# Pooled keys and left-over attention of batches 2 to 7 turned through DRAM and VectorE blocks

## The chip, the cores and the metric

The kernel runs on one core of one Trainium2 chip (trn2). The metric is the device time of one execution in microseconds (us). The core's engines are TensorE (PE, matmuls and the turning of 128x128 blocks; PEld is its loading of weights), VectorE (DVE), ScalarE (ACT), GpSimd (POOL) and SyncE (SP, which only issues DMAs). Each engine takes its own instructions in order; semaphores hold one back until what it reads is there.

## What is computed

q, k and v have 8 batches, 8 heads, 576 positions and 64 numbers a head. Keys and values are pooled by eight to 72, then softmax attention, and its output (576 x 512 a batch) goes through a gated MLP whose gate mixes positions.

```python
k_p = k.reshape(B, H, Sp, pool, D).mean(axis=3)      # pool = 8, Sp = 72
v_p = v.reshape(B, H, Sp, pool, D).mean(axis=3)
attn = softmax(q @ k_p.T / sqrt(D))                  # with + 1e-09 under the fraction
x = (attn @ v_p)                                     # heads side by side: 576 x 512
h = gelu_tanh(x @ w_in); u, v = h[..., :512], h[..., 512:]
v_s = w_sg @ (layer_norm(v) * g_ln) + b_sg
out = x + (u * v_s) @ w_out
```

## The kernel before, in words

The work of a batch is cut into steps named by a letter, each a Python generator (one function `step_X`); every call of it gives out the instructions up to its next `yield`. Which call comes when is written out by hand in four tables of tokens, `PROLOGUE`, `FIRST`, `PERIOD` and `LAST` (lines 23 to 69): `T1+1` is the next call of step T, group 1, of the batch after the one that the table stands for. `PERIOD` is run for batches 2 to 6, `FIRST` for 1 and `LAST` for 7 (lines 955 to 959). A token of a step that is already through gives out nothing. The order of the tokens is the order of every engine's instructions, DMA issues on SP's queue included (lines 961 to 966).

The steps, for batch b and group g or part i:

- A, B load k and v (`load_kv`, line 314), E loads the eight left-over positions of each head's 72 pooled ones (`load_left`, line 334), C loads q (`load_q`, line 348), each as several DMAs on SP's queue.
- K0 and K1 sum k by eight (line 396, tile `kp`), K2 sums the left-overs (tile `lp`), then turns `kp` with two and `lp` with one 128x128 transpose on TensorE into PSUM (lines 420 and 422) and scales the result into `kbd` on ScalarE (lines 430 and 431). P does the values.
- Q turns q in 32x32 blocks on VectorE (line 501), from a tile `qraw` into a tile `qT`, two of each.
- S multiplies q with `kbd` (line 514), takes the maximum, the exponentials and the sum and divides; GpSimd then copies the columns of the left-over keys into `el` (line 564).
- T turns the 128 main columns with five transposes on TensorE (helper `turn`, line 161), ScalarE rounds the result to `ah` (line 600) and VectorE makes the rest `al` (line 607). L does the same with the 64 columns of `el`: five transposes, four copies of 32x576 (line 580), two subtractions (line 587), into `lt`.
- V multiplies attention with the values (eight matmuls), H is the v half and U the u half of the first MLP matrix, W the mixing of positions (28 matmuls of 288 columns), G the combinations for a product scheme of batches 1 to 6, O the second matrix (in those batches seven products of 12 matmuls, each followed by VectorE's addition, line 841), Z turns the output and stores it.

Matmul operands are split into a rounded part and the rest; all matmuls of the steps stand at line 126. PSUM has four buffers, taken with `take()` and given back with `give()`; a step that takes one waits for the instruction that last read it.

Of the kernel before, what the change touches and what calls it, by code (L numbers as in the profile page):

```python
# [40 lines left out]
S2+0 H1+0 r0 S2+1 V0+0 S1-15 r0 V2+0 Q0+2 P2+1 P2+0 S3+1 W1-12 W0-11 r0 Z2-1 S3+1 r0 P2+1 S2-9 r0 r1 H1+0 H3+0 H3+0
O3-1 H2+0 Z1-1 r1 H3+0 P0-2 H1+0 O3-1 W0-6 H2+0 S3+1 H4+0 H4+0 O3-1 r1 S2+1 H0+0 H3+0 H2+0 H4+0 H2+0 r1 U2+0 Z3-1 H1+0
H3+0 H0+0 P2+1 P1-2 S3+1 S1-1 r3 C1+2 H1+0 H3+0 H4+0 Z3-1 H0+0 H4+0 U3+0 S1+1 S3+1 W1-1 H1+0 H4+0 U1+0 U2+0 Z2-1 H0+0
V1-21 U1+0 W0-17 E0+2 H4+0 U0+0 K0+2 S2+0 H0+0 U3+0 H4+0 H0+0 K1+2 r3 W1+0 W0+0 W1+0 A1-3 U0+0 T0+1 W0+0 r3 r3 L0+1
# [946 lines left out]
```

## Time and profile before

| what | value |
|---|---|
| runs (us) | 557.1, 557.34, 558.71; median 557.34 |
| the profiled execution, span from its first to its last instruction | 554.8 us |
| its own time beside the span | not given on the page; the runs' median lies 2.5 us over the span |
| TensorE | 542.7 us busy, 98% of the span, 3753 matmuls |
| VectorE, ScalarE, GpSimd | 415.6, 374.5 and 307.3 us busy |
| DMA | 46.34 MB, nearly all from SP's queue |
| granted TensorE clock | 1.00 in every slice of the span |

Matmuls are pipelined: the listed duration of one (298 ns for 288 columns) overlaps with that of the next, so the cost of a group is read from one start to the next start. The time of an engine that another one waits for is read from the lists of waits and the chain of work that ended last, the share of busy time is an average over all stages.

### The profile page before, as it was taken

Reading aid. Unit: us, or ns where it says so; the run is one execution under the profiler, and the core shown is the slowest. Engines: PE = TensorE matmul, PEld = TensorE weight load, DVE = VectorE, ACT = ScalarE, POOL = GpSimd, SP = SyncE. Lnnn points to the kernel's source line nnn. Section 1 sums busy time; section 2 is a strip of 40 time slices with the busy share of each in tenths; the row PEclk is TensorE's granted clock in tenths of the full one; section 3 lists DMA queues with packets and bytes.
Section 4 is the critical chain, followed back from the end, with each engine's and each line's share of the span. In section 5 each row is a group of like instructions: output and inputs, shape, how many; then the busy total and the mean of one; then the engine's idle time right before and its main releaser. Section 6 shows DMA issues by size and latency. Waiting matters only on the chain.

```text
span 554.8 us, 10369 instructions
## 1 busy us (share of the span) xinstructions
PE 542.7 (98%) x3753; PEld 513.9 (93%) x3753; DVE 415.6 (75%) x592; ACT 374.5 (68%) x981; POOL 307.3 (55%) x365
## 2 busy tenths in 40 slices
...
PEclk9999999999999999999999999999999999999999
...
GB/s 251 326 220 218 190 66 55 54 128 63 98 1 78 116 22 106 24 108 108 12 117 43 68 107 90 40 77 116 24 108 22 108 1 1 1 42 45 2 1 86
DMA packets 161603, 46.34 MB, mean 84 GB/s; under 512 B 149072, under 2 KB 149072, under 8 KB 161552
## 3 DMA queue, kind: packets, MB, share of 16 engines
...
q8 instruction: 29, 0.48, 0.4%
q14 instruction: 22, 0.18, 0.1%
...
## 4 chain that ended last, share of the span: by engine, by line
PE 65%; DVE 11%; ACT 6%; issue 1%; POOL 1%; DVEq 0%
PE ps L126 62%; PE ps L161 3%; ACT e L538 2%; DVE e L556 1%; DVE vk L694 1%; DVE nmax L519 1%; DVE kp L396 1%; DVE bst L683 1%; ACT L709 1%; ACT L538 1%; DVE xmem L689 1%; ACT xmem L678 1%; DVE qT L501 1%; DVE vbl L476 1%; DVE left L673 0%
## 5 line engine op out<-in xcount | busy, mean ns | idle before, releaser
L126 PE MATMUL ps<-wsh,vk 128*128 128x288 f32 x512 | 97.8, 298 | 1.4 <-DVE al L607 1.4
L126 PE MATMUL ps<-xhlk,wih 128*128 128x288 f32 x512 | 89.9, 298 | 0.0
L126 PE MATMUL ps<-wih,xhlk 128*128 128x512 f32 x256 | 84.6, 398 | 0.0
L126 PEld LDWEIGHTS ps<-wsh,vk 128*128 128x128 f32 x512 | 77.9, 188 | 2.2 <-PE ps L126 2.2
L126 PEld LDWEIGHTS ps<-xhlk,wih 128*128 128x128 f32 x512 | 75.6, 189 | 0.9
L538 ACT ACTIVATE e<-ps,nmax 128x72 f32<-128x72 f32 x240 | 73.0, 338 | 0.2
L694 POOL TENSOR_TENSOR vk<-xmem,vk 128x512 fp32r<-128x512 f32 x32 | 43.4, 1369 | 43.5 <-DVE nmax L519 24.8
L126 PEld LDWEIGHTS ps<-wih,xhlk 128*128 128x128 f32 x256 | 48.1, 188 | 10.7
L126 PE MATMUL ps<-wsl,vk 128*128 128x288 f32 x256 | 57.4, 295 | 0.0
L126 PE MATMUL ps<-xhlk,wil 128*128 128x288 f32 x256 | 55.0, 296 | 0.0
L538 ACT ACTIVATION_READ_ACCUMULATOR e<-ps,nmax 128x1 f32 x240 | 54.0, 225 | 0.0
L841 DVE TENSOR_TENSOR xmem<-ps,xmem 128x576 f32<-128x576 f32 x42 | 31.5, 755 | 26.8 <-PE ps L126 26.6
L126 PE MATMUL ps<-wil,xhlk 128*128 128x512 f32 x128 | 50.5, 395 | 0.0
L639 POOL TENSOR_TENSOR xhlk<-xmem,xhlk 128x576 fp32r<-128x576 f32 x32 | 45.4, 1434 | 1.9 <-ACT xhlk L637 1.5
L126 PE MATMUL ps<-gk,woh 128*128 128x288 f32 x224 | 46.3, 298 | 0.0
L686 POOL TENSOR_TENSOR rstd<-mv,eps 128x1 f32<-128x1 f32 (+1 forms) x40 | 7.9, 197 | 68.8 <-DVE ssum L547 35.7
L126 PE MATMUL ps<-kbd,qT 128*128 128x144 f32 x320 | 44.6, 287 | 1.1 <-ACT qT L496 0.8
L126 PEld LDWEIGHTS ps<-kbd,qT 128*128 128x128 f32 x320 | 42.2, 190 | 2.7 <-ACT qT L496 1.0
L126 PEld LDWEIGHTS ps<-wsl,vk 128*128 128x128 f32 x256 | 42.2, 188 | 0.0
L126 PEld LDWEIGHTS ps<-xhlk,wil 128*128 128x128 f32 x256 | 41.1, 188 | 0.0
L771 POOL TENSOR_TENSOR vk<-umem,vk 128x576 fp32r<-128x576 f32 x24 | 34.1, 1422 | 10.2 <-ACT vk L769 10.2
L785 POOL TENSOR_TENSOR umem<-umem 128x576 f32<-128x576 f32 x24 | 34.3, 1433 | 9.2 <-DVE umem L755 8.3
...
## 6 DMA issues: line engine op xcount, KB each, us to landing
...
```

The source lines that it names most:

```text
L126: nc.tensor.matmul(o, lhsT, rhs, start=start, stop=stop, **flags)
L161: nc.tensor.transpose(ps[:rows, i * P:(i + 1) * P], src(i), ident if i < NT - 1 else swap)
L396: nc.vector.tensor_reduce(out=o, in_=t.rearrange("p a (r d) -> p a d r", r=POOL), axis=AX.X, op=ALU.add)
L476: nc.vector.scalar_tensor_tensor(vbl[r, :, D * h:D * h + D], vp[r], 1.0 / POOL, vbh[r, :, D * h:D * h + D].bitcast(F32), op0=ALU.mult, op1 ...
L501: nc.vector.transpose(qT, st.pop(("q", b, g)).rearrange("p a i -> p (a i)"))
L538: nc.scalar.activation(e[:, i, h], slots[i][:, h], AF.Exp, bias=nmax[:, i, h:h + 1], **acc)
L639: nc.gpsimd.tensor_tensor(xhl[:, 1, g], x32[:, g], xhl[:, 0, g].bitcast(F32), op=ALU.subtract)
L686: nc.gpsimd.tensor_tensor(rstd, mv[:, 1:2], eps[:n, 1:2], op=ALU.add)
L694: (nc.gpsimd if i < NT - 1 else nc.vector).tensor_tensor(lo, vg, hi.bitcast(F32), op=ALU.subtract)
L771: nc.gpsimd.tensor_tensor(lo, x, hi.bitcast(F32), op=ALU.subtract)
L785: nc.gpsimd.tensor_tensor(x, p, q, op=ALU.subtract)
L841: nc.vector.tensor_tensor(x, ps[:, :, 0:HALF], x, op=ALU.add)
```

## The change

For batches 2 to 7 (`KEYS_TE` and `LEFT_TE` name the two batches that stay as they were) the turns of `kp`, `lp` and `el` on TensorE are left out. The tile is stored to DRAM, loaded back so that 32x32 blocks lie as VectorE's block transpose needs them, and turned there. K2 then has two stores, four loads, one VectorE transpose of 128x288 and the same scalings, from SBUF; it has five calls in place of three. L has two stores, two loads, one VectorE transpose of 96x576, the same four copies on ScalarE, and its two subtractions go to GpSimd; it has six calls in place of four. Neither takes a PSUM buffer any more. The tile that comes back from DRAM in K2 lies in the buffer of `el`.

To make room, q is loaded and turned in place in three buffers (`qbuf`), where there were two raw and two turned ones, and the constant `apart` lies in the first columns of `bbc`, which is loaded once `apart` is no longer needed.

All four tables are written anew. The first five lines of `PROLOGUE` and the first seven tokens of the sixth are the same. In the diff the other tables are left out but for `PERIOD`.

```diff
 PERIOD = """
...
+S1+1 H0+0 V0+0 C3+1 S0+1 Q2+1 H0+0 H2+0 S1+1 V2+0 V3+0 H2+0 H0+0 V1+0 S0+1 S1+1 H3+0 H0+0 H4+0 H4+0 H2+0 U0+0 P1+1
+H0+0 H4+0 H2+0 S1+1 S1+1 H1+0 H3+0 H0+0 P0+1 Q3+1 H4+0 S2+1 H1+0 U0+0 T0+1 H2+0 S2+1 H1+0 A1+2 T0+1 H3+0 S0+1 S3+1
+U1+0 S3+1 T0+1 H4+0 S2+1 S2+1 C0+2 A0+2 H1+0 S3+1 H1+0 H3+0 S3+1 U2+0 P2+1 H3+0 H4+0 U3+0 S2+1 H4+0 H2+0 H4+0 H1+0
+U3+0 S3+1 H3+0 W1+0 U1+0 K0+2 P2+1 U2+0 L0+1 W1+0 W0+0 P2+1 L0+1 W0+0 B0+2 K1+2 G1+0 W3+0 L0+1 G0+0 W2+0 G0+0 P2+1
+L0+1 W3+0 G1+0 E0+2 L0+1 W2+0 L0+1 G1+0 T1+1 G2+0 G2+0 V0+1 T1+1 T2+1 T1+1 O0+0 V1+1 G2+0 G3+0 V0+1 O1+0 C1+2 G4+0
+K2+2 T2+1 T2+1 G2+0 V2+1 O0+0 V1+1 G3+0 G2+0 Q0+2 K2+2 G3+0 T3+1 K2+2 Q1+2 B1+2 O0+0 T3+1 T3+1 W1-5 G4+0 C2+2 V3+1
+W0-4 O0+0 G4+0 O0+0 O0+0 V1+1 V3+1 O2+0 G4+0 O1+0 K2+2 V2+1 O2+0 G4+0 O1+0 K2+2 O1+0 Z1+0 V0+1 V2+1 S0+2 S0+2 Z1+0
+V3+1 Z0+0 O0+0 O0+0 Z3+0 Z0+0 Z2+0 Z2+0 Z3+0
 """.split()
 """.split()
...
@@ -99,11 +96,19 @@
     REC_SB = ((0, 0), (0, 1), (0, 2), (0, 3))
     MUL_POOL = ((0, 0), (0, 1), (0, 2), (0, 3))
     LO_W = ()
+    KEYS_TE = (0, 1)
+    LEFT_TE = (0, 1)
     W_POOL = ()
 
     const = ctx.enter_context(tc.tile_pool(name="const", bufs=1))
     per = ctx.enter_context(tc.tile_pool(name="per", bufs=1))
     psum = ctx.enter_context(tc.tile_pool(name="psum", bufs=1, space=bass.MemoryType.PSUM))
+
+    dram = ctx.enter_context(tc.tile_pool(name="dram", bufs=1, space=bass.MemoryType.DRAM))
+
+    fark = [dram.tile([9 * 32, P], F32, name=f"fark{n}") for n in range(2)]
+
+    farl = [dram.tile([S, H * JL], F32, name=f"farl{n}") for n in range(2)]
 
     turns = {}
 
@@ -130,7 +135,8 @@
     nc.vector.memset(kbd, 0.0)
     ident = const.tile([P, P], F32, name="ident")
     make_identity(nc, ident)
-    apart = const.tile([P, P], F32, name="apart")
+    bbc = const.tile([P, S], F32, name="bbc")
+    apart = bbc[:, 0:P]
     nc.gpsimd.tensor_copy(apart.rearrange("p (a j) -> p a j", a=2), ident.rearrange("p (j a) -> p a j", a=2))
     mhalf = const.tile([P, 1], F32, name="mhalf")
     nc.gpsimd.memset(mhalf, -0.5)
@@ -170,8 +176,11 @@
     wth = const.tile([P, S], F32R, name="wth")
     wtl = const.tile([P, S], F32R, name="wtl")
     nc.gpsimd.memset(wtl.bitcast(F32)[TAIL:2 * TAIL], 0.0)
-    bbc = const.tile([P, S], F32, name="bbc")
     gcol = const.tile([P, DF2 // P], F32, name="gcol")
+
+    eraw = const.tile([96, S], F32, name="eraw")
+    nc.gpsimd.memset(eraw[32:64], 0.0)
+    qbuf = const.tile([P, 3, S], F32, name="qbuf")
 
     st = {}
 
@@ -356,7 +365,7 @@
                 load(t[:, :, h], q[b, 2 * g + h].rearrange("(t p) d -> p t d", t=6))
             st["q", b, g] = t
             return
-        t = per.tile([P, S // 32, 32], F32, name="qraw", tag=f"qraw{g % 2}")
+        t = qbuf[:, (G * b + g) % 3].rearrange("p (k i) -> p k i", i=32)
         for h in range(2):
             sv = q[b, 2 * g + h].rearrange("(t j) (f i) -> f j t i", j=32, i=32)
             for f in range(2):
@@ -415,21 +424,38 @@
         psum8(lp[r], st["left", b][r], "left", b)
         yield
         kp = st.pop(("kp", b))
+        if b not in KEYS_TE:
+            back = fark[b % 2]
+            load(back[0:2 * P].rearrange("(a p) c -> p a c", p=P), kp.rearrange("p (a h) d -> p a (h d)", h=2))
+            load(back[2 * P:2 * P + 32], lp[96:P].rearrange("p h d -> p (h d)"))
+            yield
+            kt = per.tile([P, 9, 32], F32, name="kt", tag="el")
+            for f in range(4):
+                load(kt[32 * f:32 * f + 32], back.rearrange("(k j) c -> j k c", j=32)[:, :, 32 * f:32 * f + 32])
+            yield
+            kt = kt.rearrange("p k i -> p (k i)")
+            nc.vector.transpose(kt, kt)
+            yield
+            scale_k(b, kt[:, 0:2 * P], kt[:, 2 * P:])
+            return
         bank, ps = take()
         for a in range(2):
             nc.tensor.transpose(ps[:, 0, P * a:P * (a + 1)],
                                 kp[:, 2 * a:2 * a + 2].rearrange("p h d -> p (h d)"), ident)
         nc.tensor.transpose(ps[:, 1, 0:P], lp.rearrange("p h d -> p (h d)"), ident)
         yield
-        main = ps[:, 0, 0:2 * P].rearrange(*(("p (a l j) -> p a l j",) if b in BY_PE else ("p (a j l) -> p a l j",)), a=2, l=2)
+        scale_k(b, ps[:, 0, 0:2 * P], ps[:, 1, 96:P])
+        give(bank)
+
+    def scale_k(b, main, rest):
+        main = main.rearrange(*(("p (a l j) -> p a l j",) if b in BY_PE else ("p (a j l) -> p a l j",)), a=2, l=2)
         split_k = kbd.rearrange("p (a l) c -> p a l c", l=2)
-        rest = ps[:, 1, 96:P].rearrange("p (j g) -> p g j", g=G)
+        rest = rest.rearrange("p (j g) -> p g j", g=G)
         c = D ** -0.5 / POOL
         for h in range(2):
             r = slice(D * h, D * h + D)
             nc.scalar.mul(split_k[r, :, :, JL + JM * h:JL + JM * (h + 1)], main[r], c)
             nc.scalar.mul(kbd[r, :, LEFT[h]:LEFT[h] + JL], rest[r], c)
-        give(bank)
 
 
     vb = {b: vraw[:, 2 * (NT - 1) * DF2:].bitcast(F32).rearrange("p (g n) -> p g n", g=G) for b in WHOLE}
@@ -484,7 +510,7 @@
         st["vl", b] = vl
 
     def step_Q(b, g):
-        qT = per.tile([P, S], F32, name="qT", tag=f"qT{g % 2}")
+        qT = qbuf[:, (G * b + g) % 3]
         if b in NATURAL:
             t = st.pop(("q", b, g))
             n = S // 6
@@ -498,7 +524,8 @@
             give(bank)
             st["qT", b, g] = qT
             return
-        nc.vector.transpose(qT, st.pop(("q", b, g)).rearrange("p a i -> p (a i)"))
+        st.pop(("q", b, g))
+        nc.vector.transpose(qT, qT)
         st["qT", b, g] = qT
         yield
 
@@ -566,6 +593,28 @@
 
     def step_L(b, _):
         el = st.pop(("el", b))
+        if b not in LEFT_TE:
+            back = farl[b % 2]
+            n = (NT - 1) * P
+            load(back[0:n].rearrange("(t p) k -> p t k", p=P), el[:, 0:NT - 1])
+            load(back[n:S], el[P - TAIL:P, NT - 1])
+            yield
+            raw = eraw.rearrange("p (k i) -> p k i", i=32)
+            for gp in range(2):
+                load(raw[64 * gp:64 * gp + 32], back.rearrange("(k i) n -> i k n", i=32)[:, :, 32 * gp:32 * gp + 32])
+            yield
+            nc.vector.transpose(eraw, eraw)
+            yield
+            src = [eraw[64 * gp:64 * gp + 32] for gp in range(2)]
+            for gp in range(2):
+                lt = st["lt", b, gp] = per.tile([96, S], F32R, name="lt", tag=f"lt{gp}")
+                for c in (0, 2):
+                    nc.scalar.copy(lt[32 * c:32 * c + 32], src[gp])
+            for gp in range(2):
+                yield
+                lt = st["lt", b, gp]
+                nc.gpsimd.tensor_tensor(lt[32:64], src[gp], lt[64 * gp:64 * gp + 32].bitcast(F32), op=ALU.subtract)
+            return
         bank, ps = take()
         ps = ps.rearrange("p a n -> p (a n)")
         turn(ps, lambda i: el[:, i])
```

## Rows read from the trace of the kernel before

**Rows 1.** The page, busy time of each engine and the granted clock in 40 slices.
```profile
PE 542.7 (98%) x3753; PEld 513.9 (93%) x3753; DVE 415.6 (75%) x592; ACT 374.5 (68%) x981; POOL 307.3 (55%) x365
...
PEclk9999999999999999999999999999999999999999
```

**Rows 2.** Busy time by stretch: from:to, length, then each engine's busy us (instructions), clock, DMA share.
```profile
0.00:30.00 30.00, 24.79 (x182) 22.01 (x182) 22.73 (x34) 17.54 (x31) 17.77 (x38) 1.00 1.00 296
...
100.00:154.00 54.00, 54.00 (x369) 51.18 (x368) 41.45 (x56) 36.27 (x121) 38.29 (x44) 1.00 0.42 83
...
248.60:313.40 64.80, 64.47 (x451) 61.51 (x450) 50.08 (x70) 47.69 (x138) 33.21 (x38) 1.00 0.37 74
...
500.00:554.80 54.80, 49.79 (x334) 46.95 (x332) 26.38 (x50) 13.06 (x27) 15.30 (x22) 1.00 0.22 33
```

**Rows 3.** Who waited for whom, TensorE, 184 to 443 us: total, times, longest.
```profile
PE ps L126 <- DVE al L607: 1.4, 4, 0.4
```

**Rows 4.** The chain that ended last, 280 to 290 us: start, us, what.
```profile
280.76 0.55 PE ps L161 x5
281.31 3.73 PE ps L126 x28
285.04 0.22 PE ps L420 x2
285.26 0.11 PE ps L422
```

**Rows 5.** Groups by line and form, VectorE and ScalarE: busy us, mean ns | idle before.
```profile
L396 DVE TENSOR_REDUCE lp<-left 64x128 f32<-64x1024 f32 x7 | 14.2, 2027 | 0.2
L501 DVE STREAM_TRANSPOSE qT<-qraw 128x576 f32<-128x576 f32 x28 | 21.3, 764 | 0.0
L587 DVE TENSOR_TENSOR lt<-ps,lt 32x576 fp32r<-32x576 f32 x14 | 10.5, 748 | 4.0 <-ACT lt L580 3.9
L607 DVE TENSOR_TENSOR al<-ps,ah 128x576 fp32r<-128x576 f32 x28 | 21.0, 751 | 13.2 <-ACT ah L600 12.0 <-POOL wbk L771 1.2
L841 DVE TENSOR_TENSOR xmem<-ps,xmem 128x576 f32<-128x576 f32 x42 | 31.5, 755 | 26.8 <-PE ps L126 26.6
L882 DVE STREAM_TRANSPOSE ylast<-xmem 128x288 f32<-128x288 f32 x8 | 3.8, 479 | 0.3
...
L430 ACT ACTIVATE kbd<-ps 64x256 f32<-64x256 f32 x16 | 6.0, 378 | 4.5 <-PE ps L422 4.4
L431 ACT ACTIVATE kbd<-ps 64x32 f32<-64x32 f32 x16 | 2.9, 179 | 0.0
L580 ACT CAST lt<-ps 32x576 fp32r<-32x576 f32 x28 | 17.6, 630 | 11.2 <-PE ps L161 10.8
L600 ACT CAST ah<-ps 128x576 fp32r<-128x576 f32 x28 | 17.9, 639 | 9.6 <-PE ps L161 6.3 <-PE ps L126 2.9
```

**Rows 6.** GpSimd: one group by line, and its timeline from 287 to 306 us.
```profile
L468 POOL TENSOR_TENSOR left<-lp,mask 32x512 f32<-32x512 f32 x7 | 7.2, 1035 | 0.5
...
287.89 1.44 POOL L771 TENSOR_TENSOR gk<-umem,gk 128x576 fp32r<-128x576 f32 x1 [1.78 <-ACT gk L769]
...
300.64 4.33 POOL L639 TENSOR_TENSOR xhlk<-xmem,xhlk 128x576 fp32r<-128x576 f32 x3
```

**Rows 7.** Timelines of SyncE's DMA issues and of VectorE, 303 to 313 us.
```profile
303.04 1.07 SPq L211 DMA_DIRECT2D out<-umem  x2
...
309.93 2.16 SPq L211 DMA_DIRECT2D qraw<-in_q  x4
...
305.67 0.78 DVE L919 STREAM_TRANSPOSE umem<-xmem 128x576 f32<-128x576 f32 x1 [0.38 <-DMA out<-umem]
```

**Rows 8.** TensorE's timeline, 290 to 294 us: start, us, engine, line, operation.
```profile
290.47 0.38 PE L126 MATMUL ps<-ah,vbh 128*128 128x288 f32 x1
...
291.62 1.76 PE L126 MATMUL ps<-gk,wck 128*128 128x288 f32 x12
293.22 0.30 PE L126 MATMUL ps<-ah,vbh 128*128 128x288 f32 x1
```

More of the change, by code (lines that the diff above doesn't have):

```diff
@@ L38 @@
-Z0+0 S0+2 V2+1 A0+3 V3+1 o3 H2+1 T0+2 Z1+0 P2+2 A1+3 V3+1 S2+2 O2+0 H2+1
+T2+0 K2+1 K2+1 B0+1 V3+0 Q1+1 v2 V1+0 S0+1 V2+0 V0+0 P1+1 S1+1 S0+1 V3+0 v2 V2+0 lo0 S0+1 S1+1 u0 S1+1 S0+1 lu1 u0
+S0+1 V0+0 S1+1 V3+0 V2+0 H1+0 H1+0 S0+1 u1 V2+0 V1+0 H0+0 u1 H3+0 H0+0 V0+0 S1+1 C3+1 C0+2 V3+0 P0+1 u0 S0+1 S1+1 A1+2
+u1 u0 u0 H0+0 u2 S1+1 H1+0 H0+0 Q3+1 H4+0 H2+0 C2+1 u3 u2 H3+0 H4+0 u3 P2+1 T0+1 H4+0 u2 S3+1 U0+0 H1+0 H0+0 H2+0 u3
+u2 T0+1 A0+2 H3+0 S3+1 C2+2 Q2+1 H4+0 H4+0 u3 u2 S0+1 U0+0 H2+0 P2+1 S2+1 H4+0 P2+1 T0+1 S2+1 U1+0 P2+1 u3 H1+0 S2+1
@@ new lines @@
+H4+0 o0 o0 H3+0 S3+1 H2+0 U1+0 S2+1 H3+0 H1+0 lo1 o0 S1+1 H2+0 S2+1 S2+1 H4+0 o1 U2+0 S2+1 E0+2 K0+2 S3+1 U2+0 H0+0
+H2+0 S3+1 H3+0 K1+2 o0 o1 S3+1 U3+0 W3+0 o0 S3+1 o2 K2+2 W0+0 lb0 S2+1 K2+2 B1+2 o2 o1 S3+1 U3+0 L0+1 L0+1 o1 W3+0
+L0+1 W1+0 L0+1 o1 o3 T1+1 W0+0 V0+1 T1+1 V0+1 o3 o2 K2+2 K2+2 o3 T1+1 K2+2 W2+0 V1+1 W3+0 o2 W0+0 Q0+2 o3 T2+1 W1+0
+W2+0 C1+2 W3+0 W1+0 B0+2 W0+0 T2+1 T2+1 S0+2 S0+2 C3+2 T3+1 W2+0 W1+0 V1+1 V2+1 T3+1 W2+0 Q2+2 Q1+2 T3+1 V2+1 P1+2
+P0+2 O0+0 O0+0 S1+2 O0+0 o2 S1+2 Z0+0 Q3+2 O2+0 O2+0 S0+2 O2+0 O1+0 o3 S1+2 S0+2 V3+1 S2+2 V3+1 A0+3 A1+3 V1+1 S1+2
@@ L39 @@
+V0+1 T0+2 Z0+0 O1+0 V2+1 S2+2 V3+1 O1+0 Z1+0 H2+1 S2+2 H2+1 S0+2 C0+3 V1+1 P2+2 V3+1
 """.split()
 FIRST = """
[L41 to L44, printed above, removed]
@@ new lines @@
+H0+0 H1+0 Z3-1 U2+0 K0+2 r1 V0+0 H4+0 H0+0 H4+0 r3 H4+0 W1-1 H2+0 P2+1 Z2-1 H3+0 U3+0 H4+0 r3 S3+1 P2+1 C1+2 H0+0 U2+0
+H3+0 Z3-1 H3+0 U1+0 Q0+2 H3+0 L0+1 H0+0 K1+2 r3 r3 E0+2 Z2-1 T0+1 H0+0 H1+0 H0+0 H4+0 U3+0 K2+2 H1+0 H2+0 H2+0 L0+1
+U1+0 B1+2 H4+0 H3+0 H4+0 U0+0 L0+1 U0+0 H3+0 L0+1 H4+0 r2 L0+1 r2 L0+1 W1+0 W1+0 r2 W0+0 r2 W0+0 r2 G1+0 G0+0 K2+2
+W2+0 T0+1 W2+0 W3+0 G0+0 V0+1 W3+0 G1+0 S0+1 G2+0 T1+1 G1+0 O0+0 T1+1 V0+1 T2+1 T1+1 G4+0 V1+1 B0+2 G2+0 G2+0 O0+0
+T2+1 G2+0 G3+0 K2+2 T2+1 S2+0 O1+0 G2+0 K2+2 V1+1 S1+0 V2+1 Q1+2 T3+1 O0+0 G3+0 T3+1 T3+1 V2+1 O0+0 G3+0 V3+1 O0+0
@@ L65 @@
[L65 to L68 removed]
+V2+0 U1+0 H1+0 H3+0 H0+0 H3+0 S1+0 H0+0 H2+0 H1+0 L0-2 V1+0 T3-7 V0+0 V3+0 H2+0 T0+0 Q2+0 H3+0 H1+0 H3+0 H1+0 H1+0
```

36 lines of the change are left out of this document (7 added, 29 removed).

## Prediction

> **What bounds the kernel now.** I read the engine totals first [rows 1]: TensorE (PE) is busy for 542.7 of 554.8 us, VectorE for 75%, ScalarE 68%, GpSimd 55%. The share alone doesn't bind a stage, so next the stretches [rows 2]. In each batch period of some 64.7 us PE lacks only 0.33 us (64.80 less 64.47); from 100 to 154 us it lacks nothing. Only the opening (30.00 less 24.79 us) and the last stretch (54.80 less 49.79) have idle PE, and these are the loads before the first work and the stores after the last matmul. The list of waits says the same: over four periods PE waited only four times, 1.4 us together, for VectorE's subtraction of step T, which frees a PSUM bank [rows 3]. So between the opening and the last matmul time is PE's issue order, and an instruction taken off PE is worth its distance to the next one, not its listed duration (which overlaps with its neighbours).
>
> The granted clock is 1.00 throughout, 2.4 GHz [rows 1, 2]; nothing here is priced at the other level.
>
> **The change part by part.**
>
> *Turns taken off PE.* In the chain of waits one L is 0.55 us for its five transposes, and the two of the pooled keys and the one of the left-over keys (step K2) take 0.22 and 0.11 [rows 4]. That is 0.88 us a batch, and six batches (2 to 7) lose both: 6 x 0.88 = **-5.28 us**, all of it on the path, since PE is dense around them. No other matmul is added or removed; the 48 must be missing from PE's count.
>
> *Left-over attention through DRAM.* Per batch: SP issues two stores of `el`, two loads back; VectorE makes one 96x576 block transpose; ScalarE's four copies stay (0.63 us each [rows 5], now from SBUF); the two subtractions of 0.75 us leave VectorE [rows 5] and become two of GpSimd. The transpose is bounded by the 128x576 ones, 0.76, and by zero below; I take 0.76 [rows 5], since its columns agree. GpSimd's subtraction has no row with 32 partitions and 576 elements; 1.04 (32x512) and 1.43 us (128x576) are the ends [rows 6], I take 1.43 for the same reason. SP: a DMA issue in short runs takes 2.16/4 = 0.54 us, and a VectorE instruction that waited for the stores of `out` started at 305.67, 2.1 us after the second of the two issues (303.04 + 0.54 = 303.58) had begun [rows 7]. I take the same for a load, whose landing no row shows alone; its bounds are 0.5 (its issue) and, with the other loads of its four in front of it, 2 x 2.1. So from the last copy into `el`: 0.54 + 2.1 until the stores are in DRAM, 0.54 + 2.1 until the loads are back, 5.3 us. In the new period table the stores stand before W0, the block transpose after W3, thus two W later; a W is 28 matmuls, 3.73 us [rows 4], 7.5 us. The 5.3 us fit, with 2 us over. After the transpose 4 x 0.63 (ScalarE) and 1.43 (GpSimd) run beside W2, T1 and the rest of the W. I cost the part at nothing; its cover is W0, W3 and W2, and if that is gone, V0 waits, and H behind it.
>
> *Pooled keys through DRAM.* Per batch: two stores, four loads, a block transpose of 128x288 (0.48 [rows 5], the same form), and the four scalings on ScalarE that stay: 2 x 0.38 + 2 x 0.18 = 1.11 us [rows 5]. From the start of the reduction of the left-overs (2.03 us): 2.03 + (0.54 + 2.1) + (3 x 0.54 + 2.1) + 0.48 + 1.11 = 9.98 us until `kbd` is ready for S0. In the new order that reduction waits on VectorE behind T1's subtraction: 0.64 + 0.75 us after T1's turns [rows 5], so 11.4 us from these turns. Between them and S0 of the next batch PE has four V (290.47 to 291.62, 1.15 each), six products of O (291.62 to 293.22, 1.60 each) and T2 and T3 (0.55 each): 15.3 us [rows 4, 8]. So **the way through DRAM has some 4 us over**. What is tight is another thing: the block transpose stands on VectorE behind two gathers, and the earlier of them waits for the third product of O0. From that product's end PE has two products, 3.2 us; VectorE and ScalarE need 2 x 0.755 + 0.48 + 1.11 = 3.1 us [rows 5] and three hand-overs between engines, which no row prices alone. The bounds are 0 (the 3.2 hold) and 0.5 us a batch (three times the 0.16 by which a product's modelled end, 291.62 + 1.76, lies behind the next start at 293.22 [rows 8]); I take 0.3 for the four periods that have it (keys of batches 4 to 7): **+1.2 us**.
>
> *SP's queue.* Ten issues more a batch, 5.4 us at 0.54. The 44 it issues now (8 for k and v, 16 for q, 4 for the left-overs, 16 for `out`) make 24 us of a 64.7 us period at that price [rows 7], so there is room. While SP waits for the stores of the keys to land, B1, C2 and the stores of Z stand behind it; the next Q and P that need them come over 10 us later. Cost nothing; cover: these loads' lead.
>
> *The order of the rest.* The only wait PE has in a period, 0.35 us [rows 3], comes from a W that takes the bank of T0 right after it. In the new table U1, U2 and U3 stand between T0 and W1, 3 x 24 matmuls, over 9 us by W's 28 in 3.73, so this goes: **-1.4 us** (bounds -1.4 and 0). L and K2 also take no PSUM bank any more.
>
> *Buffers.* q is turned in place in three slots in place of two raw and two turned; a slot comes free when S of three groups before has run, and each load stands at least a product, an S and an H of PE work behind that. `apart` now lies in `bbc`, whose load is issued later, in front of the first W's scaling. It must be there when W3 of batch 0 is scaled, and that is ordered only after W0 and L0 have been given to PE, 4.3 us behind W3's own end [rows 4]. Nothing, at most one wait of the 2.1 us of a landing [rows 7].
>
> *Opening and end.* The opening's order is the same in the first five lines of the table. At the end O2's second half, its gather, its transpose and the stores come last in both tables; the 5.0 us after the last matmul [rows 2] stay.
>
> *Elsewhere.* GpSimd gets 17 us more over six batches, in a stretch in which it ran without a gap from 287.89 to 304.97 [rows 6]; the table is new everywhere. I add **+0.5 us** for small waits (bounds 0 and 1.6, which is 0.3 in each of five periods with the opening's; beyond that it is the second rival).
>
> Sum: -5.28 + 1.2 - 1.4 + 0.5 = **-5.0 us**. The page gives the profiled execution's span alone, 554.8; the median of the runs, 557.34, is 2.6 us above it, and I let that lie around the span unchanged. So 549.8 for the span, **552.3 us** for the run.
>
> **The rivals.**
>
> *Keys late from DRAM (slower).* If the store's data can be read back only much later than the 2.1 us that [rows 7] show for a store to `out`, S0 waits for `kbd`, once a period, four times, and everything on PE behind it. There are 4 us of room, the gain without it is 5 us; above 5.3 us extra per round trip it is a loss, e.g. 2 x 3.5 us extra, 3.0 us late four times, +12 - 5 = +7: 564. For it: no row shows a load of what was just stored, and stores and loads back share SP's queue with q's and k's loads. Against: the store has a row at 2 us, and the upper bound taken for a load, 2.1 us more, still fits into the room. From about 1.7 us late in a period the kernel is slower beyond what a measurement can tell. Chance 0.10.
>
> *The saved time returns as waits (no change).* VectorE and GpSimd are tight behind W: with L's two subtractions there are 17 GpSimd instructions of 1.43 us from the first G to the last V of a batch, 24.3 us, against 24.9 us of PE work there (W3 and W2 2 x 3.73, T1 0.55, the 15.3 and a last product of 1.60). One us late a period for six batches eats the gain: 557. The Trainium skill, "VectorE: DVE Perf Modes", section "Rules for kernel authors", bears on this: it puts a 128x128 transpose on TensorE where PSUM will do as its destination, as it did here. By that rule the time would not fall. The rows speak against it in this kernel: PE is the engine with nothing over, 0.88 us a batch, and the others have a quarter or more. Chance 0.12, 0.01 of it that the branch is not taken and PE's count stays.
>
> *All tight places hold (faster still).* -5.28 - 1.4 and no new wait: 550.7. Part of the forecast's range.
>
> **How the numbers follow.** About 0.3% (1.7 us) is what a measurement of this kernel can tell from no change. Forecast with its bounds (550.7, and 557.3 - 5.3 + 2.0 + 1.6 = 555.6): 0.78, all of it faster. Same 0.12, slower 0.10. The range of 8 in 10 runs from 550.5 to 556.8: the bounds of the unknown terms and half of the case of no change; the slower case and the rest stay outside.
>
> **What would show it.** PE's count falls by 48; the turns of `el` and those of L420 and L422 fall to a quarter. PE's idle per period is 0.3 us or less, period length 63.9 us. VectorE gets rows for 96x576 and 128x288 transposes near 0.77 and 0.48. Waits of PE for ScalarE `kbd` below 0.4 us each. Wrong, if PE waits over 1 us for `kbd` or for `lt`, if SP's waits for the stores to DRAM are far above 2 us, or if GpSimd is what PE waits for.

## The result, and the profile after

The changed kernel takes 565.61 us (median of 4 runs, 564.66 to 567.26) where the kernel before, run beside it, takes 557.75: the ratio is 1.0144, interval 1.0123 to 1.0166. (Ratios and intervals here are taken over all runs of both kernels, so they differ a little from the quotient of the medians.) It is 8 us slower; the prediction said 5 us faster. The profiled execution took 564.9 us, its span 563.1.

The page's engine totals after, with the granted clock:

```profile
PE 545.9 (97%) x3705; PEld 512.1 (91%) x3705; DVE 417.3 (74%) x592; ACT 374.1 (66%) x979; POOL 324.0 (58%) x378
...
PEclk9999999999999999999999999999999999999999
```

The 48 turns are gone (3753 matmuls in [rows 1]), GpSimd has its 17 us more. A slice of the clock row is 14 us long, so the 3.4 us at half clock that come up below do not show in it. Next the stretches of the changed kernel (columns as in [rows 2]):

```profile
60.00:100.00 40.00, 35.74 (x263) 34.40 (x262) 38.52 (x53) 28.89 (x49) 26.34 (x33) 1.00 0.38 90
...
140.00:180.00 40.00, 37.36 (x266) 36.32 (x264) 25.38 (x28) 18.51 (x31) 29.76 (x24) 0.96 0.21 44
245.88:310.12 64.24, 64.18 (x442) 60.65 (x441) 49.18 (x70) 47.90 (x137) 35.79 (x41) 1.00 0.42 84
```

and two of them in the kernel before:

```profile
60.00:100.00 40.00, 39.52 (x303) 39.12 (x302) 39.08 (x56) 31.85 (x53) 27.10 (x34) 1.00 0.36 90
140.00:180.00 40.00, 40.00 (x293) 39.08 (x292) 26.28 (x32) 23.02 (x54) 29.04 (x21) 1.00 0.34 61
```

Two holes are new: between 60 and 100 us TensorE (PE) starts 263 matmuls instead of 303, and between 140 and 180 us 266 instead of 293. The period is 64.24 us, 0.5 shorter than the 64.75 of before; the turns alone are 0.88.

Busy time hides short waits, since listed matmuls overlap. So in the table below PE's loss is worked out from the starts: for each matmul the distance to the next one's start, less the median distance for its size in the periods before (0.133 us for 288 columns, 0.233 for 512, 0.122 for 144, 0.109 for a transposition), summed by stretch of the profiled execution.

| kernel | matmuls | 0-60 us | 60-100 | 140-180 | 180-440 | 440-end | median of its runs |
|---|---|---|---|---|---|---|---|
| before | 3753 | 12.1 | 1.0 | 0.1 | 2.7 | 0.6 | 557.75 |
| after | 3705 | 13.4 | 5.9 | 5.4 | 4.2 | 1.7 | 565.61 |

48 turns less are 48 x 0.109 = 5.2 us; the five columns add 1.3 + 4.9 + 5.3 + 1.5 + 1.1 = 14.1, and what follows the last matmul is 0.7 us shorter (4.54 us instead of 5.26): 8.2 of the 8.3 us by which the spans differ. The 1.3 us of the first column can't be put down to the change: one and the same order of the opening lost 12.6 and 17.1 us there in two of the experiments below (PE waited 0.7 us for a load of q in the first and 3.3 in the second, and the second ran at half clock from 21.71 to 28.54 us).

TensorE's waits, whole span (the lines left out lie in the first 30 us or are under 0.7 us):

```profile
PE ps L131 <- DVE vk L743: 2.4, 1, 2.4
PE ps L131 <- DVE e L583: 1.8, 1, 1.8
...
PE ps L131 <- DVE left L722: 1.2, 1, 1.2
PE ps L131 <- DVE lt L636: 0.7, 1, 0.7
```

All four are for VectorE and stand between 62 and 152 us. None is for `kbd` in a period, and the `lt` is one of a batch whose left-overs stay on TensorE. From 184 to 443 us, where [rows 3] had four waits, PE has none in the list; its weight loads have these:

```profile
PEld ps L131 <- DVE al L656: 2.2, 12, 0.2
PEld ps L131 <- DVE xmem L890: 1.2, 4, 0.3
```

The new operations cost what was said. Groups by line of the changed kernel, then SP's waits for the stores to DRAM:

```profile
L606 DVE STREAM_TRANSPOSE eraw<-eraw 96x576 f32<-96x576 f32 x6 | 4.6, 771 | 0.0
L437 DVE STREAM_TRANSPOSE kt<-kt 128x288 f32<-128x288 f32 x6 | 2.8, 468 | 0.0
...
L616 POOL TENSOR_TENSOR lt<-eraw,lt 32x576 fp32r<-32x576 f32 x12 | 17.0, 1414 | 7.1 <-ACT lt L612 2.4 <-POOL gk L820 2.3 <-issue 2.2
```

```profile
SPq L220 <- DMA farl<-el: 6.1, 5, 1.2
SPq L220 <- DMA fark<-lp: 4.9, 5, 1.1
```

0.77 and 0.47 us for the block transposes, 1.41 for GpSimd's subtraction; VectorE waits for neither load (no idle time in front of its transposes). The round trip is in time. So where do the two holes come from? VectorE's timeline of the changed kernel around the second one, then GpSimd's:

```profile
144.60 2.02 DVE L405 TENSOR_REDUCE lp<-left 64x128 f32<-64x1024 f32 x1
146.66 4.04 DVE L738 TENSOR_SCALAR left<-left,mv,rstd 64x512 f32<-64x512 f32 x1
150.62 0.76 DVE L606 STREAM_TRANSPOSE eraw<-eraw 96x576 f32<-96x576 f32 x1
151.41 0.69 DVE L743 TENSOR_TENSOR vk<-left,vk 64x512 fp32r<-64x512 f32 x1
...
145.43 3.76 POOL L743 TENSOR_TENSOR vk<-xmem,vk 128x512 fp32r<-128x512 f32 x3
149.16 1.26 POOL L861 TENSOR_TENSOR sums<-wol 128x512 f32<-128x512 f32 x1
```

The normalisation of the last 64 rows (`left`, step H4 of batch 1) takes 4.04 us; other instances take 0.53. It starts as the first of GpSimd's row of four instructions ends, lies beside the other three, and ends 0.3 us after the last. W1 of batch 1 needs what follows it, PE waits 2.4 us, and the granted clock then shows 0.50 (1.2 GHz) for 3.42 us, which costs PE 1.5 us more:

```profile
153.60:157.02 3.42, 3.42 (x17) 3.42 (x16) 0.98 (x2) 0.91 (x2) 3.18 (x4) 0.50 0.02 5
```

### The profile page after: what moved, and what is told of

The parts are those of the page before. It is cut to its first block, busy times and chain, and to the rows that moved or that the text cites. A ratio compares the mean times of both kernels' runs of the same rounds, so it can differ in the third digit from the quotient of the medians.

```text
span 563.1 us, 10511 instructions
## 1 busy us (share of the span) xinstructions
PE 545.9 (97%) x3705; PEld 512.1 (91%) x3705; DVE 417.3 (74%) x592; ACT 374.1 (66%) x979; POOL 324.0 (58%) x378
## 4 chain that ended last, share of the span: by engine, by line
PE 77%; DVE 15%; DMA 3%; ACT 2%; issue 1%; POOL 1%; SPq 1%; DVEq 0%; POOLq 0%
PE ps L131 74%; PE ps L167 3%; DMA kvraw<-in_k 2%; DVE xmem L890 2%; DVE left L738 2%; DVE e L556 1%; DVE nmax L546 1%; DVE xmem L738 1%; DVE kp L405 1%; DVE ssum L568 1%; DVE tops L268 1%; DVE bst L732 1%; DMA kvraw<-in_v 1%; SPq L220 1%; DVE vp L405 1%
## 5 line engine op out<-in xcount | busy, mean ns | idle before, releaser
L131 PEld LDWEIGHTS ps<-wsh,vk 128*128 128x128 f32 x512 | 79.2, 191 | 3.4 <-DVE e L583 2.0
L565 ACT ACTIVATION_READ_ACCUMULATOR e<-ps,nmax 128x1 f32 x240 | 56.7, 236 | 0.0
L131 PE MATMUL ps<-kbd,qbuf 128*128 128x144 f32 x320 | 44.8, 287 | 2.0 <-ACT qbuf L522 1.5
L131 PEld LDWEIGHTS ps<-kbd,qbuf 128*128 128x128 f32 x320 | 41.7, 190 | 3.5 <-ACT qbuf L522 1.9
L743 POOL TENSOR_TENSOR vk<-xmem,vk 128x512 fp32r<-128x512 f32 x32 | 41.4, 1306 | 1.5 <-ACT vk L741 1.5
L802 DVE SCALAR_TENSOR_TENSOR ps<-ps,gcol,bbc 128x576 f32<-128x576 f32 x28 | 23.1, 824 | 21.4 <-PE ps L131 21.0
```

The source lines that it names most:

```text
L131: nc.tensor.matmul(o, lhsT, rhs, start=start, stop=stop, **flags)
L565: nc.scalar.activation(e[:, i, h], slots[i][:, h], AF.Exp, bias=nmax[:, i, h:h + 1], **acc)
L743: (nc.gpsimd if i < NT - 1 else nc.vector).tensor_tensor(lo, vg, hi.bitcast(F32), op=ALU.subtract)
L802: nc.vector.scalar_tensor_tensor(vs, vs, gcol[:, d:d + 1], bbc.rearrange("p (a n) -> p a n", a=2), op0=ALU.mult, op1=ALU.add)
```

## The experiments

Two theories stood at the start. **A**: the new order of issue lost the time, in the opening; the turn through DRAM is a gain inside it. **B**: the turn itself lost it, by its round trips, its transfers or GpSimd's subtractions. The state of all steps at the start of PERIOD is the same in both tables, so openings and periods can be exchanged.

### Order alone

The changed order with all turns on TensorE.

```diff
-    KEYS_TE = (0, 1)
-    LEFT_TE = (0, 1)
+    KEYS_TE = tuple(range(B))
+    LEFT_TE = tuple(range(B))
...
+        if b > 1:
+            yield
+            yield
+            yield
         bank, ps = take()
         for a in range(2):
...
+        if b > 1:
+            yield
+            yield
         bank, ps = take()
         ps = ps.rearrange("p a n -> p (a n)")
         turn(ps, lambda i: el[:, i])
```

> The changed kernel's order of issue throughout, with all turns of batches 2 to 7 back on TensorE (each where VectorE's block transposition stood; the three of the keys and their scaling together at the scaling's place) and the left-over subtractions back on VectorE. Theory A (the new order of issue lost the time, and the turn through DRAM is a gain inside it): 48 transposes return, 5.3 us, so 568.5 to 571, above the changed kernel's 565.6. Theory B (the turn itself lost the time, by its round trips, its transfers or its GpSimd subtractions): back near the kernel before, 556 to 560.

Measured: 578.8 us, ratio 1.0381 (1.0363 to 1.0398). B is out: with nothing through DRAM the kernel is slower still, and PE loses 6.2 us at 60 to 100 us and 6.1 at 140 to 180, so both holes are there. It is also 8 us slower than A said, and part of that is this experiment's own: the keys' turn stands with its scaling right ahead of S0, and PE waits for the scaling in each period (184 to 443 us):

```profile
PE ps L131 <- ACT kbd L463: 4.1, 4, 1.0
```

Since neither part comes apart here, the size of the gain is read from the next ones.

### Openings and periods exchanged

`old_opening`: the changed kernel with PROLOGUE and FIRST of before (`C3+1` moved behind the next `S0+1`), `KEYS_TE = (0, 1, 2, 3)`, `LEFT_TE = (0, 1, 2)`.

> The changed kernel with PROLOGUE and FIRST of the kernel before (one load of queries moved behind the scores whose buffer it takes), so that keys of batches 4 to 7 and left-overs of batches 3 to 7 still go through DRAM, in the new PERIOD and LAST; those of the opening stay on TensorE. Theory A: the 557.75 of before, less 4 x 0.33 and 5 x 0.55 us of turns (4.1), plus the 1.6 us of new small waits that the steady periods of the changed kernel show, about 1 us for the end: 554.5 to 557, faster than before. Theory B: nine of the twelve turns are still there, so at least 562.

`old_prologue`: with PROLOGUE of before alone, `KEYS_TE = (0, 1, 2)`.

> The changed kernel with only PROLOGUE of the kernel before; FIRST, PERIOD and LAST are the new ones (keys of batch 2 turn on TensorE). Theory A: the 5.0 us lost between 60 and 100 us (and perhaps the 1.3 us before) go, the 5.4 us lost between 140 and 160 us around the late value tail of batch 1 stay if FIRST alone makes them: 559 to 561; if that loss hangs on what PROLOGUE left behind, 555 to 557. Theory B: 563 to 566.

`new_opening`: with PERIOD and LAST of before, `KEYS_TE = (0, 1, 4, 5, 6, 7)`, `LEFT_TE = (0, 1, 3, 4, 5, 6, 7)`.

> The changed kernel with PERIOD and LAST of the kernel before: new PROLOGUE and FIRST with three turns through DRAM (keys of batches 2 and 3, left-overs of batch 2), all later turns on TensorE in the old order. Theory A: 557.75 plus the 11 us lost up to 160 us in the changed kernel, less 1.2 us of turns: 565 to 568. Theory B: three turns of twelve, so about a quarter of the loss: 558 to 560.

| kernel | matmuls | 0-60 us | 60-100 | 140-180 | 180-440 | 440-end | median | ratio to before |
|---|---|---|---|---|---|---|---|---|
| old_opening | 3716 | 12.6 | 1.0 | 0.1 | 4.3 | 1.8 | 555.32 | 0.9974 (0.995 to 0.9997) |
| old_prologue | 3708 | 16.1 | 0.9 | 4.0 | 4.3 | 1.7 | 560.96 | 1.006 (1.0043 to 1.0076) |
| new_opening | 3742 | 13.6 | 6.7 | 5.1 | 3.0 | 0.6 | 568.17 | 1.0185 (1.0154 to 1.0217) |

A's ranges hold in the first two, and in the third the median is 0.2 us above its range; B's are missed in all three. The hole at 60 to 100 us belongs to the new PROLOGUE, that at 140 to 180 us to the new FIRST, and each goes with its table alone. The new opening with the old periods is worse than the whole change; the new periods behind the old opening are faster than the kernel before, with nine of the twelve turns through DRAM.

### What held the normalisation

Two explanations of the hole in FIRST: GpSimd's row holds the VectorE instruction (**port theory**), or it is only late in VectorE's queue. First the forms by themselves, eight kinds of VectorE instructions alone and beside GpSimd, in one run:

> A kernel by itself that leaves out the whole computation: eight forms of VectorE instructions as they stand in the kernel, each run in a row once with GpSimd idle and once beside six GpSimd subtractions of 128x512 in SBUF back to back (about 8 us of them). Port theory (what the trace of the changed kernel suggests): the normalisation 64x512 from SBUF to SBUF takes 0.53 us alone, and beside GpSimd one of them lasts until GpSimd's row ends, 4 us or more; the same for 128x512 and for the integer merge with two SBUF inputs (0.69 alone); the reduction (2.0), the block transposition (0.77), the statistics (0.66) and the subtraction with a PSUM input (0.72) stay as they are. Rival (VectorE was late only because of what was queued ahead, and the 4.04 us is not GpSimd's doing): every form takes the same time alone and beside.

VectorE's timeline, for each form first alone, then beside GpSimd, and GpSimd's row beside the 128x512 normalisation (not shown for VectorE), beside the merge and beside the form with an input in PSUM:

```profile
8.53 2.25 DVE L42 TENSOR_SCALAR left<-left,mv,one 64x512 f32<-64x512 f32 x4
...
13.70 5.76 DVE L42 TENSOR_SCALAR left<-left,mv,one 64x512 f32<-64x512 f32 x4
...
34.12 2.86 DVE L48 SCALAR_TENSOR_TENSOR top<-high,top 128x512 int32<-128x512 int32 x4
...
39.89 5.68 DVE L48 SCALAR_TENSOR_TENSOR top<-high,top 128x512 int32<-128x512 int32 x4
...
63.12 3.13 DVE L54 TENSOR_TENSOR al<-ps,ah 128x576 fp32r<-128x576 f32 x4
...
69.16 3.12 DVE L54 TENSOR_TENSOR al<-ps,ah 128x576 fp32r<-128x576 f32 x4
...
76.06 3.77 DVE L57 TENSOR_REDUCE kp<-kv 128x128 f32<-128x1024 f32 x2
...
82.74 3.82 DVE L57 TENSOR_REDUCE kp<-kv 128x128 f32<-128x1024 f32 x2
...
25.31 8.09 POOL L70 TENSOR_TENSOR gc<-ga,gb 128x512 f32<-128x512 f32 x6
...
38.69 9.22 POOL L70 TENSOR_TENSOR gc<-ga,gb 128x512 f32<-128x512 f32 x6
...
67.96 7.37 POOL L70 TENSOR_TENSOR gc<-ga,gb 128x512 f32<-128x512 f32 x6
```

Four normalisations take 5.76 us beside GpSimd instead of 2.25, four merges of two SBUF inputs 5.68 instead of 2.86 (the subtraction of two SBUF tiles the same); with an input in PSUM, and for the reduction, nothing changes, nor for the block transposition and the statistics. One point fell: no instruction was held to the end of the row. The normalisations took 1.36 to 1.56 us each; of the merges the first, which started before GpSimd's row, took 0.68 and the others 1.63: the two engines took turns, one instruction each. Why one instruction in the kernel is held through three stays open. It is not the only one: in the changed kernel's trace the normalisation of the last batch's tail took 4.00 us through a row of three (527.01 us), and in the kernel before one took 2.76 through two (517.55 us); each ended 0.3 us after GpSimd's row.

This is what the Trainium skill says in "SBUF — State Buffer", section "Who interferes with whom": VectorE and GpSimd share one pair of SBUF ports, VectorE's two-port modes (its tensor_scalar among the forms) and its instructions with two SBUF inputs need it, and who comes second waits for the other's instruction. The forms agree, with the numbers above; the hold in the kernel, 4.04 us through three GpSimd instructions, is longer than the one instruction of that rule.

Then the kernel. `sums_later`, an edit that moves nothing but GpSimd's order in FIRST:

```diff
-... H4+0 r2 L0+1 r2 L0+1 W1+0 W1+0 r2 ...
+... H4+0 L0+1 L0+1 r2 r2 W1+0 W1+0 r2 ...
```

> The changed kernel with one edit in FIRST: the first GpSimd instruction of the third sum of output weights (1.26 us at 149.16, back to back behind three value subtractions) is issued behind the two left-over subtractions. Nothing on VectorE, ScalarE or TensorE moves. Port theory: the normalisation at 146.66 ends with GpSimd's row, now at 149.2 instead of 150.4, so it takes 2.8 us instead of 4.0, TensorE's wait falls from 2.5 to 1.3 us: 563 to 564.7. Rival (order on VectorE alone): the normalisation and the wait are as they were, 565 to 566.5.

Measured 563.22 us, ratio 1.0105 (1.0081 to 1.0128). VectorE and GpSimd in its timeline, and PE's wait:

```profile
147.18 2.81 DVE L738 TENSOR_SCALAR left<-left,mv,rstd 64x512 f32<-64x512 f32 x1
...
145.94 3.77 POOL L743 TENSOR_TENSOR vk<-xmem,vk 128x512 fp32r<-128x512 f32 x3
```

```profile
PE ps L131 <- DVE vk L743: 1.2, 1, 1.2
```

2.81 us where 2.8 was said, a wait of 1.2 where 1.3 was said, and the loss at 140 to 180 us is 2.9 instead of 5.4. So GpSimd's row is what holds the instruction: with two of its instructions left in place of three, the hold is shorter by one. That the shared ports are the way it does so rests on which forms are touched, and on the section of the Trainium skill above. The wait alone gives 1.2 us of the 2.5; the rest is the half clock, which does not show behind the shorter wait (this trace has it at 79.18 to 82.59 us instead). Behind the same wait of 2.4 us it shows in `new_opening` and `no_u_pool` too, for 3.41 us, and not in `old_prologue` (loss there 4.0): a wait of that length may bring the lower level, and need not.

`tail_on_act`, the other way round, gives ScalarE the instruction:

```diff
+        if i == NT - 1:
+            nmr = per.tile([P, 1], F32, name="nmr", tag="nmr")[:n]
+            nc.gpsimd.tensor_tensor(nmr, tiny[:n, 0, 0:1], mv[:, 0:1], op=ALU.subtract)
+            nc.gpsimd.tensor_tensor(nmr, nmr, rstd, op=ALU.mult)
         yield
-        nc.vector.tensor_scalar(vg, vg, mv[:, 0:1], rstd, op0=ALU.subtract, op1=ALU.mult)
+        if i == NT - 1:
+            nc.scalar.activation(vg, vg, AF.Identity, bias=nmr, scale=rstd)
+        else:
+            nc.vector.tensor_scalar(vg, vg, mv[:, 0:1], rstd, op0=ALU.subtract, op1=ALU.mult)
```

> The changed kernel with one edit: the normalisation of the last 64 rows of the values (H4, the instruction that took 4.04 us at 146.66) is done by ScalarE with scale and bias, for all batches, with two GpSimd instructions of 64x1 more. Port theory: the wait of 2.5 us of TensorE for the value tail of batch 1 shrinks to 1.5 us at most (where the subtraction behind is held in its place) or goes, and the stretch of half clock behind it with it: 561 to 564. Rival (the tail is late because keys' reduction and left-over block stand ahead of it on VectorE): the tail is not earlier by more than the 0.5 us that leave VectorE: 565 to 566.

Measured 563.26 us, ratio 1.0105 (1.0084 to 1.0126). The hold moved to the next instruction with two SBUF inputs, which now starts under the same row:

```profile
147.65 3.58 DVE L750 TENSOR_TENSOR vk<-left,vk 64x512 fp32r<-64x512 f32 x1 [0.36 <-ACT vk L748]
```

PE's wait is 1.2 us again, as the bound of 1.5 allowed. No run took the hold in FIRST away whole: both edits leave half of the wait. `old_opening_act` puts this edit on `old_opening`:

> The two together: PROLOGUE and FIRST of before, the new PERIOD and LAST, and the normalisation of the last 64 rows on ScalarE in all batches. Port theory: the hold of the last batch (4.0 us at 527 in the changed kernel) goes too, which costs TensorE about 0.5 us there: 554 to 555.3, against 555.3 without the edit and 557.7 before. Rival: the ScalarE queue is the tighter one, and its 0.6 us more a batch cost 0.5 us each: 556 to 559.

555.6 us (12 runs), ratio 0.9974 (0.9955 to 0.9992): no gain over `old_opening`. Its hold of 4.0 us in the last batch had cost TensorE almost nothing (0.2 us), and GpSimd's own row is now later there (500 to 556 us), 0.4 us by the two small instructions more and 0.4 by VectorE's subtraction, which takes a turn in it here (1.11 us) and lengthens a GpSimd instruction from 1.28 to 1.71:

```profile
PE ps L132 <- POOL vk L751: 1.0, 1, 1.0
```

### The hole of PROLOGUE

VectorE is busy for 39.1 of 40 us there before, and for 38.5 after. `lighter` takes work off it: groups 0 and 1 of batch 1 leave `SOFTMAX`.

> The changed kernel with one edit: the softmax of groups 0 and 1 of batch 1 goes the way of batches 2 to 7 (twenty exponentials with sums on ScalarE in place of an addition, one exponential and a summing reduction), which takes 2 x 1.8 us off VectorE and puts 2 x 2.3 us on ScalarE, near 65 to 85 us. If VectorE's queue is what makes TensorE late in the new PROLOGUE (9.8 of 10 us busy there), TensorE's loss of 5.9 us between 60 and 100 us falls to 3 or less: 562 to 564. Rival (ScalarE or the order of PSUM banks is as tight): 565 to 568.

574.92 us, ratio 1.0312 (1.0289 to 1.0336): a miss that tells nothing of PROLOGUE's hole. The loss between 60 and 100 us fell only from 5.9 to 5.0, and ahead of it, between 40 and 60 us, PE lost 9 us more than in the changed kernel, 6.8 of them in a wait for GpSimd's low part of `x`, and the clock is at 0.50 from 52.01 to 58.84 us. In the new way GpSimd's queue has copies of `el` in front of that low part, and it stands idle for 7.92 us before them, until VectorE has made `e`: the edit did more than move work from VectorE to ScalarE. But rows of the changed kernel in that stretch look like those of FIRST. VectorE, then GpSimd:

```profile
57.76 1.42 DVE L268 SCALAR_TENSOR_TENSOR tops<-graw,tops 128x512 int32<-128x512 int32 x1
...
59.55 1.70 DVE L268 SCALAR_TENSOR_TENSOR tops<-graw,tops 128x512 int32<-128x512 int32 x1
...
61.77 1.40 DVE L738 TENSOR_SCALAR xmem<-xmem,mv,rstd 128x512 f32<-128x512 f32 x1
...
66.95 2.15 DVE L502 SCALAR_TENSOR_TENSOR vbl<-vp,vbh 64x256 fp32r<-64x256 f32 x2
...
59.40 1.29 POOL L270 TENSOR_TENSOR tops<-tops,graw 128x512 int32<-128x512 int32 x1 [0.78 <-DVE tops L268]
61.39 1.49 POOL L270 TENSOR_TENSOR tops<-tops,graw 128x512 int32<-128x512 int32 x1 [0.69 <-ACT wih L273]
...
67.10 1.28 POOL L275 TENSOR_TENSOR wil<-tops,wih 128x512 fp32r<-128x512 f32 x1
```

`no_u_pool` takes these GpSimd instructions away:

```diff
+    nc.gpsimd.memset(wil.bitcast(F32)[:, :, 0:DF2], 0.0)
...
-            nc.gpsimd.tensor_tensor(top, top, low, op=ALU.add)
+            if name != "u":
+                nc.gpsimd.tensor_tensor(top, top, low, op=ALU.add)
...
-            (nc.vector if name in LO_W else nc.gpsimd).tensor_tensor(lo, top, hi.bitcast(F32), op=ALU.subtract)
+            if name != "u":
+                nc.gpsimd.tensor_tensor(lo, top, hi.bitcast(F32), op=ALU.subtract)
```

> The changed kernel with GpSimd's eight instructions of about 1.3 us for the first half of the input weights left out (the low bits are not added and the low part of these weights is zero: that part of the computation is left out); VectorE's, ScalarE's and TensorE's instructions and all orders stay. In the changed kernel these instructions lie beside VectorE's stretched ones at 59.55 (merge of weights, 1.70 us instead of 0.69), 61.77 (normalisation, 1.40 instead of 0.5) and 66.95 (value subtraction, 1.3 us too long). Port theory: those three go back to their usual times, 3 us less on a VectorE that is 98% busy there, and TensorE's loss between 60 and 100 us falls from 5.9 to 3.5 or less: 562 to 564. Rival (the order alone makes the loss, the stretch is hidden): the loss stays at 5 to 6 us, 565 to 566.5.

562.1 us (9 runs), ratio 1.0058 (1.0025 to 1.0092). The same VectorE instructions:

```profile
57.45 1.42 DVE L269 SCALAR_TENSOR_TENSOR tops<-graw,tops 128x512 int32<-128x512 int32 x1
...
59.23 0.69 DVE L269 SCALAR_TENSOR_TENSOR tops<-graw,tops 128x512 int32<-128x512 int32 x1
...
60.45 0.53 DVE L741 TENSOR_SCALAR xmem<-xmem,mv,rstd 128x512 f32<-128x512 f32 x1
...
64.76 0.82 DVE L505 SCALAR_TENSOR_TENSOR vbl<-vp,vbh 64x256 fp32r<-64x256 f32 x2
```

Three of four are back at their usual times; the first lies beside another GpSimd instruction, which stays, and is as long as before. PE's loss between 60 and 100 us is 3.0 instead of 5.9. So 2.9 of PROLOGUE's 4.9 us hang on these GpSimd instructions, and the three VectorE durations that fell back (1.0 + 0.9 + 1.3 = 3.2 us) are as much. The edit also takes some 10 us of work off GpSimd (8 x 1.3), and no run separates that from the hold. The other 2 us are left to PROLOGUE's order, which no run took apart further.

### The turn alone, and a version that beats both

`keys_alone`: the kernel before with the keys of batches 3 to 7 through DRAM (stores and loads in one call), the tables moved only for K2:

```diff
-... V0+1 G1+0 K2+2 G1+0 O0+0 ...
+... V0+1 G1+0 G1+0 O0+0 ...
...
-... T2+1 V2+1 G4+0 G3+0 O0+0 V2+1 G4+0
+... T2+1 K2+2 V2+1 G4+0 G3+0 O0+0 V2+1 K2+2 G4+0
...
-... O0+0 B0+2 V1+1 O2+0 ...
+... O0+0 B0+2 K2+2 V1+1 O2+0 ...
```

> The kernel before with one part of the change in its own order of issue: pooled keys of batches 3 to 7 go through DRAM and VectorE's block transposition (stores and loads where the three transpositions stood, VectorE's block some 8 us and the scaling some 10 us later); keys of batches 0 to 2 and all left-overs stay on TensorE. Theory A (the turn through DRAM is a plain gain where the order gives it time): five turns of 0.33 us, 557.7 less 1.65: 555.8 to 556.6, with no wait of TensorE for the keys. Theory B (the round trip or VectorE's block holds something up even here): 557.5 to 560.

556.76 us (12 runs), ratio 0.9989 (0.997 to 1.0007): between the two ranges, and not clear of no change. In the trace the four turns of PERIOD are each worth what was said: the wait for T's subtraction stands at 210.21, 274.64, 339.07 and 403.50 us, 64.43 apart, where before it stood 64.75 apart. The fifth, batch 3 in FIRST, was late: VectorE's timeline, and PE's wait behind it (60 to 560 us):

```profile
166.32 0.48 DVE L430 STREAM_TRANSPOSE kt<-kt 128x288 f32<-128x288 f32 x1 [2.66 <-DMA kt<-fark]
```

```profile
PE ps L129 <- DVE xmem L860: 1.2, 1, 1.2
```

The reduction in front of it ended at 159.14 + 2.04 = 161.2 us, so this way through DRAM took 5.1 us, with one small store and four loads in it (the larger store had gone at 146.01 us); given less, VectorE stands for the difference with the next addition behind it. `old_ends` (the `old_opening` with LAST of before, and batch 3's keys through DRAM as here) repeats that:

> PROLOGUE, FIRST and LAST of the kernel before, only PERIOD new; keys of batches 3 to 7 and left-overs of batches 3 to 7 through DRAM. Theory A: against old_opening (555.3) one more turn off TensorE (0.33), and the 1.6 us that TensorE loses between 480 and 540 us in the new LAST (0.4 us in the old) shrink: 553.6 to 554.6, below both kernels by more than the measurement is uncertain. Rival (the end is bound by what the new PERIOD leaves behind, not by LAST's own order): 555 to 556.

557.7 us (12 runs), ratio 1.001 (0.999 to 1.003), outside both ranges: PE loses 4.0 us between 140 and 180, where VectorE waits 3.6 us for the same load, PE 2.1 us for the addition behind it, and the clock is at 0.50 from 169.98 to 173.39 us (1.6 us). Without that one, `old_first_last`:

> old_ends without its one late part: PROLOGUE, FIRST and LAST of the kernel before, PERIOD new, keys of batches 4 to 7 and left-overs of batches 3 to 7 through DRAM, keys of batch 3 on TensorE again. Theory A: old_ends lost 3.9 us between 160 and 180 us because VectorE waited 3.6 us for that one load (its profile shows it); without it, and with the old LAST, old_opening's 555.3 less 0.8: 554 to 555. Rival (something else in the old LAST costs it): 555.5 to 557.

556.0 us (8 runs, 554.3 to 557.21) against 557.88 beside it, ratio **0.9959** (0.9943 to 0.9975): faster than both kernels by an interval clear of 1, though only by 0.4%, with PROLOGUE (but for the place of `C3+1`), FIRST and LAST of before and PERIOD new. The loss between 440 us and the end is 1.0 instead of 1.8, and that at 140 to 180 us 0.1 instead of 4.0, both as A said. The median is 1 us above A's range and lies in the rival's; the profiled execution lost 14.3 us in the first 60 against 12.6 in that of `old_opening`, where the two orders are the same; its trace has half clock from 22.78 to 26.19 us (2.0 us of loss), the other has none there, so the surplus of this execution is not LAST's. Its stretches:

```profile
60.00:100.00 40.00, 39.52 (x298) 38.75 (x297) 39.07 (x56) 30.70 (x52) 27.41 (x33) 1.00 0.45 103
140.00:180.00 40.00, 40.00 (x300) 39.49 (x299) 27.26 (x32) 22.17 (x52) 30.39 (x22) 1.00 0.32 54
245.00:309.24 64.24, 64.18 (x442) 60.68 (x441) 49.29 (x70) 47.88 (x138) 35.80 (x40) 1.00 0.42 84
```

Both holes are gone, and the period is that of the changed kernel, 64.24 us.

## Why the prediction was wrong

- **Turns taken off PE, -5.28.** Right: 48 matmuls fewer, and the keys measured by themselves in `keys_alone` are worth 0.32 us a batch.
- **The round trip in time.** Right: no wait of PE for `kbd` or for a turned `lt` in any period. 5.1 us from the end of the reduction to the block transposition, where 6.4 were summed for DMA alone. It was the store that was priced high: in `keys_alone` SP issues the first load back 1.55 us after the store (161.21 to 162.76 us), where 2.64 were summed, and from there to the transposition it is 3.56 us, where 3.72 were. The three hand-overs before S0, +1.2, show no wait of PE. The rival of late keys was not the cause, but `keys_alone` and `old_ends` show it where the order leaves too little room.
- **The T0 wait, -1.4.** It went, as said. In its place came twelve waits of 0.2 and four of 0.3 us of PE's weight loads, 3.4 together. So PE's loss from 180 to 440 us rose by 1.5 us although 1.4 went, and the period fell by 0.5, not by 0.88 plus the wait of 0.35. The term "+0.5 us for small waits" was mis-sized: it came to 2.9 us there and 1.1 behind 440 us, 4.0 in all, over its bound of 1.6.
- **The step that failed: "Opening and end. The opening's order is the same in the first five lines of the table", with no price, and "from 100 to 154 us it lacks nothing" taken as lasting.** All that the sum had for the rest of the opening was its share of the "+0.5", at most 0.3 us. PROLOGUE behind its fifth line and FIRST are new, and they cost 4.9 and 5.3 us, together twice the whole gain. In PROLOGUE's stretch VectorE has nothing over (39.1 of 40 us before). In FIRST's it has (26.3 of 40), and there one held instruction in front of W1 made most of the loss, 2.4 us of waiting and 1.5 at half clock behind it. PE's full rows there were the work of the old order: with the old tables the losses are 1.0 and 0.1 us again (`old_opening`).
- **What lay under it: durations taken as fixed.** Each VectorE instruction that the prediction prices has one duration, the mean of its group, wherever it stands; the normalisation is not priced at all. The trace of before had the counter-evidence, in a row that the prediction did not use:

```profile
L689 DVE TENSOR_SCALAR left<-left,mv,rstd 64x512 f32<-64x512 f32 x8 | 8.1, 1013 | 7.0 <-POOL rstd L687 7.0
```

  A mean of 1.0 us for an instruction that takes 0.53 by itself: two of the eight were held in that kernel too, batch 1's for 2.13 us (134.56 us) and batch 7's for 2.76, at places where PE did not need them (it lost 0.1 us from 100 to 180 and 0.6 behind 440). In the changed kernel the mean is 1.4: the same two were held, for 4.04 and 4.00 us, and batch 1's is now in front of W1.
- **The rivals.** None had the new order of the opening as a cause. "The saved time returns as waits" named VectorE and GpSimd, but put the place in the periods behind W and the price at the gain. The sum was right about PERIOD's sign, not its size: in `old_first_last`, 0.9959, the gain is 2.3 us (557.75 x 0.9959 = 555.5), where the terms give 3.8 for its nine turns (4.1 + 1.4 - 1.2 - 0.5). That 555.5 lies in the predicted range is owed to the range's width.
- **The rule of the Trainium skill**, "VectorE: DVE Perf Modes", section "Rules for kernel authors" (a 128x128 transpose on TensorE where PSUM will do), is not borne out where PE is the bound: in `old_first_last` nine turns (37 transposes) moved off it and the ratio is 0.9959.
